# A fused attention and SwiGLU block: when the gate and up weight tiles are made, and where the second blocks' rows wait

## The chip, the cores and the metric

The kernel runs on one core of a Trainium2 chip. The metric is device time in microseconds of one execution; the time of a version is the median of its runs. Beside the timed runs there is one profiled execution, which all rows of the trace come from.

## What is computed

The reference is one adaptive-layer-norm transformer block in float32, with 2048 rows of width 576. Cut to what matters:

```python
mod = silu(c) @ w_mod                       # six vectors: sa, ca, ga, sb, cb, gb
h = layernorm(x) * (1 + ca) + sa
q = h @ wq                                  # 32 heads of 128
o = softmax(q k^T / sqrt(128)) v            # last 512 cached keys and values, 16 KV heads
x = x + ga * (o @ wo)                       # 4096 -> 576
h = layernorm(x) * (1 + cb) + sb
x = x + gb * ((silu(h @ w1) * (h @ w3)) @ w2)   # 576 -> 4608 -> 576
```

## The kernel before, in words

**Precision.** TensorE multiplies in a rounded float32 form. Every operand is therefore split into a high part (a rounded copy, by ScalarE) and a low part (operand minus high part, by VectorE or GpSimd), and three products stand for one. A product of 2 x 2 blocks is done with seven block products instead of eight (p1 to p7); for that, sums and differences of the blocks have to be made first.

**Stages.** First attention, in 128 slots i of four steps t (one slot is one head on one block of 512 rows; first both row blocks 0 and 1 over all heads, then blocks 2 and 3). Then the MLP's projections, `mlp()`, in 72 groups g: 36 feature tiles f of 128 columns, gate and up together, on the row blocks 0 and 1 (groups 0 to 35, the first pass), and the same tiles again on blocks 2 and 3 (groups 36 to 71, the second pass, which begins with tiles 35 and 34). A group has seven products k = 0 to 6 in the order p1, p2, p6, p7, p5, p3, p4 (line 554), each of seven matmuls. Between products PE does the down projection of the pair of groups before, in units of six matmuls: one unit after each of k = 0, 1, 2, 3 and 6, two after k = 4, none after k = 5 (line 962). Units write two PSUM banks by turns (pe, pf); VectorE adds each into SBUF (L904). A unit can only start when VectorE has drained the same bank two units earlier.

**What each product sets off.** After p1, ScalarE copies the bank y (L989) before p6 may add to it; after p6 likewise (L995); after p5 likewise (L998), and p3 waits for that. VectorE adds the second bank x (L991, L999, L1005) and multiplies (L1003, L1006). In odd groups VectorE also makes one low part of the activations at k = 5 (L110, with its high part by ScalarE, L109); the other low parts of activations (L110) and their sums (L943, L950, L958, L959) are GpSimd's.

**Weight tiles.** A tile f of gate and up has four blocks of 128 x 384. `load_raw(f)` (L667) brings them to SBUF; `set_piece(f, n)` (L673) makes the seven operands: GpSimd sums (L683 to L688), a high part by ScalarE (L692), a low part by GpSimd in two instructions (L697, L698). The finished 128 x 5 x 128 operand is written to DRAM (`put_out`, L703), and `load_wset` (L786) brings it back, in both passes, one operand per product, a group ahead (L1211 to L1216), into eight buffers. `set_piece` also serves the query weights. `r_item` does the same for the rows of w2, `h_item` for the activations of the families A0, A1, M0.

**What sets the order.** The order on each engine is the program's order, written out by hand: `at(i, t, task, ...)` puts a task after step t of slot i, or of group ("m", g); step -1 is ahead of the group's first product. All DMAs shown go through SyncE's queue, in order. Preparation is spread over attention's steps by a planner, `lay` (L1164): each item has pieces with costs in ns for GpSimd, and a piece goes to the first step whose pace (3300 or 3100 ns a step, less fixed work) leaves room. An item is loaded when the item before the last has ended, since two buffers hold raw data. A first list (37 items) starts at step 13, a second one at slot 68; into the second, the three M0 items are put at index 16.

**Row buffers.** Four wide buffers (tag "x", 9 KB a partition) hold either a block of rows, `acc[b]`, or raw weights. During the first pass all four hold rows: acc[0] and acc[1], which the down projection adds into, and acc[2] and acc[3], which are waiting. `spill(b)` writes rows to DRAM, `load_x(b)` brings them back, `fetch_rows(b)` brings them into other buffers for the layer norm. `split_x(pair)` (L1217) is one GpSimd subtraction over 128 x 1152 elements that the down projection of that pair of blocks needs beforehand. At the end of the first pass `finish` (L852) does five GpSimd sums per row tile.

Of the kernel before, what the change touches and what calls it, by code (L numbers as in the profile page):

```python
# [8 lines left out]
F32 = mybir.dt.float32  # L9
F32R = mybir.dt.float32r  # L10
# [7 lines left out]
P = 128  # L18
D = 576
DC = 4  # L20
DR = 64
# [8 lines left out]
NF = F // P  # L30
# [8 lines left out]
WLEAD = 4  # L39
PACE = 3300, 3100  # L40
MORE, A1_ITEM = 0, 3

ORDERED = {mybir.EngineType.PE, mybir.EngineType.DVE, mybir.EngineType.Activation, mybir.EngineType.Pool, mybir.EngineType.SP}
SCALE = float(DH) ** -0.5
# [8 lines left out]
def tile_block(  # L53
# [16 lines left out]
    nc = tc.nc  # L70
# [5 lines left out]
    pool = ctx.enter_context(tc.tile_pool(name="pool", bufs=2))  # L76
# [52 lines left out]
    acc, rows, mid = {}, {}, {}  # L129
# [424 lines left out]
    ORDER = ("p1", "p2", "p6", "p7", "p5", "p3", "p4")  # L554
# [6 lines left out]
    hd, hsets, sets = {}, {}, {}  # L561
# [77 lines left out]
    def load_set(fam, k):  # L639
# [4 lines left out]
    wdram = {  # L644
        (f, k): dram.tile([P, DC + 1, P], F32, name=f"wd{f}{k}")
        for f in (*range(NF), *(("q", g) for g in range(HKV)))
        for k in ORDER
    }
    works = {}
# [17 lines left out]
    def load_raw(f):  # L667

        whole = wide([P, 6, 3, P], "wraw")
        nc.sync.dma_start(whole[:, :4], w13[f] if isinstance(f, int) else wqs2[f[1]])  # L670
        works[f] = whole

    def set_piece(f, n):  # L673

        def views():
            return [works[f][:, k] for k in range(6)]

        k, which = (("p2", 1), ("p1", 0), ("p4", 3), ("p5", 4), ("p6", 5), ("p7", 2), ("p3", 1))[n]

        def prep():  # L680
            a11, a12, a21, a22, s1, s2 = views()
            if n == 0:
                nc.gpsimd.tensor_add(s1, a21, a22)  # L683
                nc.gpsimd.tensor_sub(s2, s1, a11)
            elif n == 1:
                nc.gpsimd.tensor_sub(a21, a11, a21)
            elif n == 6:
                nc.gpsimd.tensor_sub(a12, a12, s2)  # L688

        def high():  # L690
            x, t = views()[which], staging([P, DC + 1, P], "wmade")
            nc.scalar.copy(t[:, :3, :], x)  # L692
            return x, t

        def low(xt):
            x, t = xt
            nc.gpsimd.tensor_sub(t[:, 3:, :], x[:, :2, :], t[:, :2, :].bitcast(F32))  # L697
            nc.gpsimd.tensor_sub(t[DR:, 2, :], x[DR:, 2, :], t[DR:, 2, :].bitcast(F32))  # L698
            if n == 6:
                del works[f]  # L700

        def put_out(xt):
            nc.sync.dma_start(wdram[f, k][:, :, :], xt[1].bitcast(F32))  # L703

        return (0 if n == 6 else None, (2040, 1020, 0, 0, 0, 0, 1020)[n], 1200), (prep, high, low, put_out)

    DOWN = (("p4", "p7"), ("p6",), ("p1", "p5"), ("p2", "p3"))
    G = NF // 2
    FLIP, LAST = G, G - 2
# [2 lines left out]
        for p in range(G + 1)  # L712
        for q, ks in enumerate(DOWN)
    }
# [14 lines left out]
    def rows_pieces(p):  # L729
# [4 lines left out]
        def piece(n, k, which, last):  # L734
# [26 lines left out]
            def put_out(xt):  # L761
                to = []
                if k is not None:
                    q = next(q for q, ks in enumerate(DOWN) if k in ks)
                    to.append(odram[p, q][:, DOWN[q].index(k), :, :])
                if p == LAST and k in ("p1", None):
# [252 lines left out]
    def at(i, t, task, *args):  # L1019

        tasks.setdefault((i, t), []).append((task, args))
# [72 lines left out]
    for Q in range(PLAIN, 2 * HKV):  # L1094
        spans, at0 = (FIRST_SPANS, 16 * Q - 5) if Q == PLAIN else (SPANS, 16 * Q - 9)
        step = at0
        for k, counts in zip(ORDER_Q, spans):
            begin[Q, k] = step
            n0 = 0
            for c in counts:  # L1100
                qsteps.setdefault(step, []).append((Q, k, slice(n0, n0 + c)))
                n0, step = n0 + c, step + 1
# [50 lines left out]
    def w_item(f):  # L1153
        return (lambda: load_raw(f)), [set_piece(f, n) for n in range(7)]

    def r_item(p):
        return (lambda: load_rows(p)), rows_pieces(p)

    mlp_items = []
    for p in range(G + 1):  # L1160
        mlp_items += [w_item(f) for f in (2 * p, 2 * p + 1) if p < G]
        mlp_items.append(r_item(p))

    def lay(items, first, STEP):  # L1164
# [46 lines left out]
    for g in range(last_group):  # L1211
        for k, name in enumerate(ORDER):
            if groups[g][1] == groups[g + 1][1]:
                at(("m", g), k, keep_wset, g, name)
            else:
                at(("m", g), k, load_wset, g + 1, name)  # L1216
    def split_x(pair):  # L1217

        a = acc[2 * pair + 1]
        nc.gpsimd.tensor_sub(a[:, :, :HALF], a[:, :, :HALF], a[:, :, HALF:])  # L1220

    for d in range(2 * G):
        g = 2 * d
# [5 lines left out]
            times = ((4, (g, 2)), (3, (g, 4)))  # L1229
        for q, (i, t) in times:  # L1230
            at(("m", i), t, load_oset, d, q)
    for pair, i in ((0, ("m", 0)), (1, ("m", 14))):
        at(i, 0, split_x, pair)
    at(("m", 2), -1, begin_sums, 0)
    at(("m", 2 * G + 2), 3, begin_sums, 1)

# [60 lines left out]
    for b in (2, 3):  # L1297
        for t in range(ST):
            at(("m", b), t, norm_stats, b, t)
        at(("m", 4), 1, norm_root, b)  # L1300
    for b, g in ((2, 6), (3, 9)):
        at(("m", g), 0, norm_scale, b)
        for t in range(ST):
            at(("m", g), t, norm_rows, b, t)
        for m in range(DC + 1):
            at(("m", g + 1 + m // 3), 2 * (m % 3), store_h, "M1", b, m, "AS"[m % 2], "raw")
    at(("m", 12), -1, begin_parts, "M1")
    for c in range(3):
        g = 12 + 6 * c
# [104 lines left out]
    for k, name in enumerate(("shift", "gain")):  # L1414
        sections = wms.pop(k)
        for m in (2, 3, 0, 1, 4):
            w = sections[m]
# [26 lines left out]
    for m in range(DC + 1):  # L1444
        k = P if m < DC else DR
# [111 lines left out]
```

## Time and profile before

| | |
|---|---|
| median of 3 runs | 2955.62 us (2955.44 to 2955.67) |
| the profiled execution | 2954.41 us, its span 2952.6 us |
| PE busy | 2903.8 us (98%) |
| DVE, ACT, POOL busy | 2011.1, 1560.9, 1751.2 us |
| moved by DMA | 751.27 MB, 254 GB/s over the span |
| the M0 groups, from the first matmul of p1 | 1708.62 us on, most of them 16.73 us |

PE is TensorE, DVE VectorE, ACT ScalarE, POOL GpSimd, SP SyncE. A row of a timeline has the start in us, the duration, the engine, the line of the kernel, the operation and its tiles and, in brackets, how long the engine stood idle before it and what ended that. A row of a group has busy time, the mean duration in ns and the idle time ahead of the group's instructions. "x<-y" names the tile written and those read.

### The profile page before, as it was taken

What the parts mean: (1) busy time and instruction counts of PE and PEld (TensorE: products, weight loads), DVE (VectorE), ACT (ScalarE), POOL (GpSimd) and SP (SyncE); (2) the same over time, 40 slices, a digit from 0 to 9 for tenths busy, and PEclk for the clock granted to TensorE, in tenths of its full rate; (3) what the DMA queues carried; (4) which work ended last, traced back from release to release, by engine and by line L of the source; (5) the groups of instructions that cost most, each with busy time, mean ns of one, the idle gap of its engine ahead of it and who ended that gap; (6) DMA issues with size and microseconds to landing.
All of it is one profiled execution on the core that took longest, in us unless ns stands there. A gap on an engine that the chain in (4) does not pass through costs nothing.

```text
span 2952.6 us, 47355 instructions
## 1 busy us (share of the span) xinstructions
PE 2903.8 (98%) x16056; PEld 2384.8 (81%) x16056; DVE 2011.1 (68%) x3149; ACT 1560.9 (53%) x3251; POOL 1751.2 (59%) x1884
## 2 busy tenths in 40 slices
PE   7999999999999999999999999999999999999999
PEld 6777777777777777777777778888888888888887
DVE  7877787777777877777777766555555555555556
ACT  6667777777656776677677543333333222222322
POOL 3678888888712877777878223355564544334345
PEclk9999999999999999999999999999999999999999
DMA  6989999999885999989889946677766766666664
GB/s 216 280 266 347 277 345 311 298 289 299 260 277 179 326 301 295 296 284 283 273 278 299 300 154 202 218 233 251 251 226 202 286 231 199 205 198 193 202 201 143
DMA packets 441205, 751.27 MB, mean 254 GB/s; under 512 B 185730, under 2 KB 185730, under 8 KB 437380
## 3 DMA queue, kind: packets, MB, share of 16 engines
q1 hardware_dynamic: 440964, 748.25, 79.1%
q8 instruction: 128, 2.10, 0.3%
q14 instruction: 113, 0.93, 0.1%
HBM read 474.97 MB, written 235.37 MB: 241 GB/s over the span
## 4 chain that ended last, share of the span: by engine, by line
PE 80%; DVE 7%; ACT 4%; issue 2%; POOL 1%; DMA 1%; SPq 0%; ACTq 0%; POOLq 0%; DVEq 0%
PE py L797 15%; PE px L797 11%; PE po L530 10%; PE pe L428 10%; PE pf L910 7%; PE pe L910 7%; PE qy L797 5%; PE pt L505 4%; PE qx L797 3%; PE pss L466 2%; PE pss L468 2%; PE pss L467 2%; DVE nm L470 1%; DVE pt L515 1%; DVE acc L547 1%
## 5 line engine op out<-in xcount | busy, mean ns | idle before, releaser
L797 PE MATMUL py<-hset,wset 128*128 128x512 f32 x2016 | 507.2, 391 | 0.0
L547 DVE SCALAR_TENSOR_TENSOR acc<-pe,r,acc 128x576 f32<-128x576 f32 x510 | 413.6, 811 | 58.1 <-PE pe L428 55.4
L797 PEld LDWEIGHTS py<-hset,wset 128*128 128x128 f32 x2016 | 362.4, 188 | 59.0 <-ACT u L998 0.2
L428 PEld LDWEIGHTS pe<-o,oth 128*128 128x128 f32 x2040 | 319.7, 188 | 79.4 <-DVE acc L547 41.6
L797 PE MATMUL px<-hset,wset 128*128 128x512 f32 x1512 | 380.5, 391 | 0.0
L428 PE MATMUL pe<-o,oth 128*128 128x288 f32 x2040 | 360.1, 298 | 12.9 <-DVE acc L547 11.8
L530 PE MATMUL po<-pt,v 128*128 128x512 f16 x1536 | 353.8, 380 | 0.3 <-DMA v<-vs 0.3
L470 DVE TENSOR_REDUCE nm<-pss 128x1 f32<-128x512 f32 x512 | 345.6, 675 | 7.3 <-PE pss L468 7.1
L479 ACT ACTIVATE p<-pss,nm 128x512 f32<-128x512 f32 x384 | 265.7, 692 | 144.7 <-DVE nm L470 141.5
L697 POOL TENSOR_TENSOR wmade<-wraw,wmade 128x256 fp32r<-128x256 f32 x364 | 272.8, 749 | 115.5 <-issue 49.5
L110 POOL TENSOR_TENSOR akv<-u,akv 128x512 fp32r<-128x512 f32 x141 | 182.7, 1307 | 228.8 <-ACT akv L109 227.9
L797 PEld LDWEIGHTS px<-hset,wset 128*128 128x128 f32 x1512 | 275.5, 188 | 49.4
L509 ACT ACTIVATE pt<-pt 128x512 f16<-128x512 f32 x384 | 229.7, 598 | 136.6 <-PE pt L505 134.9
L535 DVE SCALAR_TENSOR_TENSOR otl<-po,undo,oth 128x512 fp32r<-128x512 f32 x128 | 96.1, 751 | 278.7 <-ACT oth L534 272.9
L515 DVE SCALAR_TENSOR_TENSOR pt<-pt 128x512 f16<-128x512 f32 x384 | 261.7, 681 | 28.7 <-ACT pt L509 28.3
L530 PEld LDWEIGHTS <-v 128*128 128x128 f16 x1536 | 140.6, 98 | 160.3 <-DMA v<-vs 0.6
L505 PEld LDWEIGHTS pt<-ident,p 128*128 128x128 f32 x1536 | 186.0, 140 | 72.0 <-PE pss L468 15.7
L505 PE MATMUL pt<-ident,p 128*128 128x128 f32 x1536 | 231.2, 273 | 9.4 <-DVE pt L515 6.4
L797 PE MATMUL qy<-hset,wset 128*128 128x512 f32 x784 | 237.0, 413 | 0.0
L466 PE MATMUL pss<-kh,qh 128*128 128x512 f32 x512 | 227.2, 444 | 6.3 <-ACT qh L109 2.2
L428 PE MATMUL pe<-o,otl 128*128 128x288 f32 x1020 | 217.5, 294 | 0.0
L468 PE MATMUL pss<-kh,ql 128*128 128x512 f32 x512 | 201.3, 393 | 0.9 <-DVE ql L110 0.9
(250 smaller groups left out, 5974.9 us busy)
## 6 DMA issues: line engine op xcount, KB each, us to landing
oset<-od SPq DMA_DIRECT2D x106, 576.0 KB, 4.7
od<-omade SPq DMA_DIRECT2D x133, 288.0 KB, 4.1
wraw<-in_B_w SPq DMA_DIRECT2D x36, 768.0 KB, 6.4
kept<-o SPq DMA_DIRECT2D x64, 288.0 KB, 5.1
o<-kept SPq DMA_DIRECT2D x32, 576.0 KB, 5.8
wraw<-in_A_wq_pairs SPq DMA_DIRECT2D x16, 768.0 KB, 6.3
w2raw<-in_B_w SPq DMA_DIRECT2D x38, 288.0 KB, 4.3
oset<-od SPq DMA_DIRECT2D x35, 288.0 KB, 3.2
```

Source lines behind the costliest of these rows:

```text
L428: nc.tensor.matmul(ps[:, h, :HALF], a[:, rows], b[:, h * HALF : (h + 1) * HALF], start=n == 0, stop=n == 2)
L466: nc.tensor.matmul(pss, st["qh"][:, rows], kh, start=True, stop=False)
L468: nc.tensor.matmul(pss, st["ql"][:, rows], kh, start=False, stop=True)
L470: nc.vector.tensor_reduce(nm, pss, axis=AX.X, op=ALU.max, negate=True)
L479: nc.scalar.activation(p, pss, AF.Exp, bias=nm, accum_out=st["l"][:, t : t + 1])
L505: nc.tensor.transpose(ps[:, j * P : (j + 1) * P], p[:, j * P : (j + 1) * P], ident)
L515: nc.vector.scalar_tensor_tensor(lo, p, LIFT, hi, op0=ALU.mult, op1=ALU.subtract)
L530: nc.tensor.matmul(po, v[:, d, j, :], pt[:, e, j, :], start=k == 0, stop=k == 3 * KC - 1)
L547: nc.vector.scalar_tensor_tensor(a, ps[:, :, :HALF], st["r"][:, t : t + 1], a, op0=ALU.mult, op1=ALU.add)
L697: nc.gpsimd.tensor_sub(t[:, 3:, :], x[:, :2, :], t[:, :2, :].bitcast(F32))
L797: nc.tensor.matmul(ps, w[:, a, :], h[:, b, :], start=start and n == 0, stop=n == 6, skip_group_check=True)
L910: nc.tensor.matmul(ps[:, h, :HALF], a[:, rows], w[:, b, :], start=m == 0, stop=m == 2)
```

## The change

The constant `MADE_LATE = 7` leaves tiles 0 to 6 with the planner. Tiles 7 to 35 are made during the first pass, a group ahead of their use: `make_high` (GpSimd sums and ScalarE's high part, straight into the SBUF buffer that PE reads) at step k of group f - 1, `make_low` one step later, now on VectorE, and `keep_set`, three steps after that, writes the operand to DRAM for the second pass (not for tile 35, which group 36 uses at once). `load_raw(f)` comes at step 4 of group f - 2. To have buffers for the raw tiles, acc[2] and acc[3] are spilled at group 4, fetched again for the norms at groups 5 and 8, and loaded back at groups 36 and 37; so the second pair's `split_x` moves from group 14 to step 5 of group 37. The planner's second list falls from 43 items to 14.

```diff
--- before.py
+++ after.py
@@ -39,6 +39,7 @@
 WLEAD = 4
 PACE = 3300, 3100
 MORE, A1_ITEM = 0, 3
+MADE_LATE = 7
 
 ORDERED = {mybir.EngineType.PE, mybir.EngineType.DVE, mybir.EngineType.Activation, mybir.EngineType.Pool, mybir.EngineType.SP}
 SCALE = float(DH) ** -0.5
@@ -703,6 +704,32 @@
             nc.sync.dma_start(wdram[f, k][:, :, :], xt[1].bitcast(F32))
 
         return (0 if n == 6 else None, (2040, 1020, 0, 0, 0, 0, 1020)[n], 1200), (prep, high, low, put_out)
+
+    def make_high(f, k):
+
+        a11, a12, a21, a22, s1, s2 = [works[f][:, j] for j in range(6)]
+        if k == "p1":
+            nc.gpsimd.tensor_add(s1, a21, a22)
+            nc.gpsimd.tensor_sub(s2, s1, a11)
+        elif k == "p2":
+            nc.gpsimd.tensor_sub(a21, a11, a21)
+        elif k == "p7":
+            nc.gpsimd.tensor_sub(a12, a12, s2)
+        x = {"p1": a11, "p2": a12, "p6": s2, "p7": a21, "p5": s1, "p3": a12, "p4": a22}[k]
+        t = sets[f, k] = pool.tile([P, DC + 1, P], F32R, tag="w", name="wset", bufs=8)
+        nc.scalar.copy(t[:, :3, :], x)
+        works[f, k] = x, t
+
+    def make_low(f, k):
+
+        x, t = works[f, k]
+        nc.vector.tensor_sub(t[:, 3:, :], x[:, :2, :], t[:, :2, :].bitcast(F32))
+        nc.vector.tensor_sub(t[DR:, 2, :], x[DR:, 2, :], t[DR:, 2, :].bitcast(F32))
+        if k == ORDER[-1]:
+            del works[f]
+
+    def keep_set(f, k):
+        nc.sync.dma_start(wdram[f, k][:, :, :], works.pop((f, k))[1].bitcast(F32))
 
     DOWN = (("p4", "p7"), ("p6",), ("p1", "p5"), ("p2", "p3"))
     G = NF // 2
@@ -1158,7 +1185,7 @@
 
     mlp_items = []
     for p in range(G + 1):
-        mlp_items += [w_item(f) for f in (2 * p, 2 * p + 1) if p < G]
+        mlp_items += [w_item(f) for f in (2 * p, 2 * p + 1) if f < MADE_LATE]
         mlp_items.append(r_item(p))
 
     def lay(items, first, STEP):
@@ -1212,8 +1239,15 @@
         for k, name in enumerate(ORDER):
             if groups[g][1] == groups[g + 1][1]:
                 at(("m", g), k, keep_wset, g, name)
+            elif MADE_LATE <= g + 1 < NF:
+                for late, task in enumerate((make_high, make_low, keep_set)[: 2 + (g + 2 < NF)]):
+                    m, step = divmod(8 * g + k + 1 + late * late, 8)
+                    at(("m", m), step - 1, task, g + 1, name)
             else:
                 at(("m", g), k, load_wset, g + 1, name)
+    for f in range(MADE_LATE, NF):
+        at(("m", f - 2), 4, load_raw, f)
+
     def split_x(pair):
 
         a = acc[2 * pair + 1]
@@ -1229,8 +1263,8 @@
             times = ((4, (g, 2)), (3, (g, 4)))
         for q, (i, t) in times:
             at(("m", i), t, load_oset, d, q)
-    for pair, i in ((0, ("m", 0)), (1, ("m", 14))):
-        at(i, 0, split_x, pair)
+    for pair, i in ((0, ("m", 0)), (1, ("m", NF + 1))):
+        at(i, 5 * pair, split_x, pair)
     at(("m", 2), -1, begin_sums, 0)
     at(("m", 2 * G + 2), 3, begin_sums, 1)
 
@@ -1298,12 +1332,16 @@
         for t in range(ST):
             at(("m", b), t, norm_stats, b, t)
         at(("m", 4), 1, norm_root, b)
+        at(("m", 4), 2, spill, b)
+        at(("m", NF + b - 2), (4, 0)[b - 2], load_x, b)
     for b, g in ((2, 6), (3, 9)):
+        at(("m", g - 1), 4, fetch_rows, b)
         at(("m", g), 0, norm_scale, b)
         for t in range(ST):
             at(("m", g), t, norm_rows, b, t)
         for m in range(DC + 1):
             at(("m", g + 1 + m // 3), 2 * (m % 3), store_h, "M1", b, m, "AS"[m % 2], "raw")
+        at(("m", g + 2), 3, rows.pop, b)
     at(("m", 12), -1, begin_parts, "M1")
     for c in range(3):
         g = 12 + 6 * c
```

## The prediction

> **What bounds the kernel now.** I read the page's head first, then busy time in stretches of 100 us, then the chain of waits for the attention half, then the engines' timelines around one group of the projections.
>
> The stretches (columns: PE with its count, weight loads, DVE, ACT, POOL, granted clock, DMA share, GB/s):
>
> ```profile
> span 2952.6 us, 47355 instructions
> 800.00:900.00 100.00, 99.62 (x563) 77.85 (x562) 75.06 (x123) 57.70 (x121) 11.72 (x8) 1.00 0.76 235
> 1500.00:1600.00 100.00, 98.91 (x559) 77.42 (x557) 74.15 (x119) 70.62 (x161) 82.03 (x109) 1.00 0.94 295
> 2100.00:2200.00 100.00, 100.00 (x546) 88.30 (x545) 55.60 (x76) 32.38 (x59) 60.31 (x46) 1.00 0.70 231
> 2600.00:2700.00 100.00, 100.00 (x546) 88.26 (x546) 54.78 (x76) 29.10 (x51) 39.68 (x30) 1.00 0.63 200
> ```
>
> PE bounds everything, at a full clock. What attention loses to preparation is small: 563 matmuls in 100 us without it (POOL 12%), 559 with it (POOL 82%). In the projections PE has no gap at all. So a change that moves POOL, ACT and DMA work can win only attention's few lost matmuls, and can lose wherever it makes the gapless PE wait.
>
> **Attention: what leaves, and what it was costing.** The rows of the chain that mark a slot's twelve matmuls with the values:
>
> ```profile
> 896.36 2.62 PE po L530 x12
> 947.68 2.62 PE po L530 x12
> ...
> 1211.73 2.62 PE po L530 x12
> 1265.92 2.62 PE po L530 x12
> ...
> 1680.01 2.62 PE po L530 x12
> ```
>
> Four slots without preparation take 947.68 - 896.36 = 51.32 us: the floor. The planner's list for the second half shrinks from 43 items to 14 (eleven row items, three of the M0 family). I worked its arithmetic through: at 3100 ns a step a row item takes five steps, so eleven from step 272 reach about 327, and the M0 items end at step 347, slot 87. Counting PE's groups of twelve, slot 68, where this list begins, has its group at 947.68, and slot 88 has it at 1211.73: from there on nothing is prepared any more. Before, the last ends at step 486, slot 121.5. The list is too short for index 16, so the M0 items come last. From 1265.92 to 1680.01 are 32 slots, 414.09 us; at the floor 8 x 51.32 = 410.56. So **-3.5 us**, and this loss has a name: DVE late in draining the output bank.
>
> ```profile
> PEld pe L428 <- DVE acc L547: 13.7, 31, 1.1
> ACT hst L1131 <- DMA hdM0p<-hst: 2.4, 1, 2.4
> PEld pt L505 <- DVE p L515: 2.2, 1, 2.2
> ```
>
> The first row covers 960 to 1680 us, the other two 1225 to 1279. The four slots from 1211.73 took 54.19, 2.9 over the floor. They hold the M0 family's last items, and ACT's wait for a staging buffer held DVE and then PE. Those items move to slots 82 to 87 and may meet the same wait there, beside fewer transfers: I take a third of it, **-1.0**; ends 0 and -2.9. In the first half three weight items become row items, of similar length: 0, with a rival below.
>
> **What comes into the first pass.** Per tile, from the rows grouped by form:
>
> ```profile
> L697 POOL TENSOR_TENSOR wmade<-wraw,wmade 128x256 fp32r<-128x256 f32 x364 | 272.8, 749 | 115.5 <-issue 49.5 <-ACT wmade L692 45.3 <-POOL wmade L698 5.4
> L692 ACT CAST wmade<-wraw 128x384 fp32r<-128x384 f32 x364 | 173.1, 512 | 2.5 <-POOL wraw L688 1.6 <-DMA od<-omade 0.6 <-POOL wmade L697 0.4
> L698 POOL TENSOR_TENSOR wmade<-wraw,wmade 64x128 fp32r<-64x128 f32 x364 | 170.2, 467 | 28.6
> L686 POOL TENSOR_TENSOR wraw<-wraw 128x384 f32<-128x384 f32 x52 | 53.2, 1023 | 1.3
> ```
>
> POOL takes four sums, 4 x 1.02 = 4.1 us per group; ACT seven casts, 7 x 0.51 = 3.6; and DVE, which did none of this before, fourteen low parts in place of POOL's 749 and 467 ns. A group lasts 16.73 us (below), so POOL goes from 10.1 busy to 14.2 while the M1 family is combined, ACT from 5.4 to 9.0. ACT's critical copy is L998 between p5 and p3, with two output units of PE over it; the casts before it have the p7 product and a unit: 0, as long as POOL's sums are a step ahead.
>
> DVE's low parts no row shows. From L1005 (0.68 us for 512 columns) and L904 (0.74 for 576), quoted next, a column costs 0.94 ns and an instruction 0.2: an estimate of 0.44 + 0.32, and 0.62 in a queue whose instructions overlap by 0.07. Seven pairs are 4.3 us on top of 0.556 x 16.73 = 9.3: 13.6 of 16.73, which fits on the average. But the place decides, and POOL. Around the start of group 30 (2225.70):
>
> ```profile
> 2224.97 1.30 POOL L958 TENSOR_TENSOR u<-u,u 128x512 f32<-128x512 f32 x1 [2.09 <-DVE u L1003]
> 2226.35 1.62 POOL L959 TENSOR_TENSOR u<-u,u 128x512 f32<-128x512 f32 x1
> ...
> 2225.58 1.23 DVE L110 TENSOR_TENSOR aal<-u,aah 128x512 fp32r<-128x512 f32 x1 [0.69 <-ACT aah L109]
> 2226.74 0.68 DVE L1005 TENSOR_TENSOR u<-px,u 128x512 f32<-128x512 f32 x1
> 2227.45 1.06 DVE L1006 TENSOR_TENSOR u<-u,s 128x512 f32<-128x512 f32 x1
> 2228.44 0.74 DVE L904 TENSOR_TENSOR acc<-pe,acc 128x576 f32<-128x576 f32 x1
> ...
> 2225.70 1.76 PE L797 MATMUL py<-hset,wset 128*128 128x512 f32 x7
> 2229.69 0.42 PE L910 MATMUL pe<-oset,aah 128*128 128x288 f32 x2
> 2242.42 1.76 PE L797 MATMUL py<-hset,wset 128*128 128x512 f32 x7
> ...
> 2243.19 0.75 DVE L904 TENSOR_TENSOR sums<-pf,sums 128x576 f32<-128x576 f32 x1
> 2246.41 0.96 PE L910 MATMUL pf<-oset,akv 128*128 128x288 f32 x6
> ...
> 2058.32 0.69 DVE L110 TENSOR_TENSOR aal<-u,aah 128x512 fp32r<-128x512 f32 x1 [0.69 <-ACT aah L109]
> ```
>
> The unit at 2229.69 writes bank pe, which L904 drains until 2228.44 + 0.74 = 2229.18: **0.5 us to spare**. In an odd group the change puts p5's low pair on DVE behind L110 (step 5), ahead of L1005, L1006 and that drain. Undisturbed that is +0.62, a stall of 0.1. But DVE work with both inputs in SBUF meets POOL's: the same L110 took 0.69 once and 1.23 here beside L958, and L959 took 1.62 against L958's 1.30, while L1005, which reads PSUM, did not stretch. So the first low part, at 2226.74, finds L959 holding SBUF until about 2227.9 and ends at 2228.2. Then POOL's two new sums for the next tile stand ready behind L959. If they miss the second low part, L1006 meets them once, the drain ends near 2230.5 and the stall is 0.85. If POOL gets in between each time, the second low part ends near 2229.2, L1006 near 2230.7, the drain near 2231.3: 1.65. I take 1.25, nearer to the blocked row, since POOL now has work queued there. It happens at 14 starts of even groups (8, 10, ... 34): 14 x 1.25 = **+17.5** (ends 14 x 0.1 = 1.4 and 14 x 1.65 = 23). At the start of an odd group (31, at 2242.42) L110 is missing and the same drain ends at 2243.94 for a unit at 2246.41, 2.5 us to spare, more than the 1.65 just worked out: 0.
>
> The Trainium skill, page "SBUF — State Buffer", section "Who interferes with whom", says that a VectorE instruction with two SBUF inputs and a GpSimd one that reads SBUF exclude each other for the whole instruction, whichever issues first. By it alone the sum takes the 1.65 and the change's low parts are in the wrong engine while POOL is busy; the rows agree that there is a block, and leave open whether it is held to the last nanosecond.
>
> **Queues and transfers.** SP gives up seven tile loads per group and gets seven stores and one raw load of 768 KB.
>
> ```profile
> DMA packets 38294, 92.82 MB, mean 232 GB/s; under 512 B 4431, under 2 KB 4431, under 8 KB 38265
> wraw<-in_B_w SPq DMA_DIRECT2D x36, 768.0 KB, 6.4
> ```
>
> From 1900 to 2300 us the first pass moves 232 GB/s; 768 KB in 16.73 us add 47, to 279, under the 295 of attention above. A store waits for a low part issued three steps earlier, so neither SP nor the output-weight loads behind it stand. The raw load is issued at step 4 of the group before and needed from step 0 of the next, three steps of 16.73 / 7 = 2.4 us, 7.2, against 6.4 to landing: 0; if it is late by 1, ACT, at 9.0 of 16.73, has room. The second blocks' rows go out at group 4, come back once for the norms and once around group 36, 2.4 MB each time, all of it several steps ahead of its first reader: 0, ends 0 and +2.
>
> **The pass boundary.** The second pair's split moves from group 14, where PE saw nothing of it, to group 37.
>
> ```profile
> L1220 POOL TENSOR_TENSOR acc<-acc x2: 2672/2682/2693, 1702.8 to 1962.9; 128x1152 f32<-128x1152 f32 x2
> ...
> 2371.12 1.27 POOL L110 TENSOR_TENSOR aal<-u,aah 128x512 fp32r<-128x512 f32 x1
> ...
> 2372.45 0.40 PE L910 MATMUL pf<-oset,aal 128*128 128x288 f32 x1 [0.87 <-POOL aal L110]
> 2373.73 0.53 PE L910 MATMUL pe<-oset,aah 128*128 128x288 f32 x2 [0.48 <-DVE acc L904]
> ```
>
> There POOL is queued without a gap from the finishing sums on, and PE already waits for it. Another 2.68 us in that queue lands on PE: **+2.7** (ends 0 and 4).
>
> Sum: -3.5 - 1.0 + 17.5 + 2.7 = +15.7. The profiled execution took 2954.41 us, its span 2952.6; it becomes 2970.1. The runs' median, 2955.62, is 1.2 above it: **2971**. A difference of 0.2%, 5.9 us, is about what I call a change.
>
> **Rivals.** (1) *Nothing to see.* The low parts find gaps in POOL, or the drain's half microsecond and a slightly cheaper low part are enough: 0.1 to 0.3 at 14 starts, 3 us. For it: 13.6 of 16.73 fits. Against it: POOL's new sums are queued just there. Then -4.5 + 3 + 2.7 = +1: 2957. (2) *Faster.* Preparation in attention costs more than the floor shows after 1212 us: the row items that replace three weight items at slots 36 to 50 load POOL and the staging buffers less. The page's total for the L428 wait on L547 is
>
> ```profile
> PEld pe L428 <- DVE acc L547: 41.6, 79, 1.2
> ```
>
> so 41.6 - 13.7 = 27.9 lie mostly before 960; over some 14 of 65 slots that is 6. If it goes, with the whole 2.9 and no stall in the first pass: -3.5 - 2.9 - 6 + 2.7 = -9.7, 2946. It decides once the 14 starts cost under 4 us together. Against it: three items of fifteen change and the pace is the same. (3) *SBUF's shared side becomes the bound.* If blocks last as long as busy times, POOL's 14.2 and DVE's two-input work (7 x 0.76 low parts, L1003, L1006 and every other L110, about 7) need 21.2 of 16.73 in the 18 groups with combining, and 0.397 x 16.73 + 4.1 + 7 = 17.7 in the other ten: 18 x 4.5 + 10 x 1.0 = +91, 3045. This is that section's rule taken to the letter. Against it: L1006 of group 31 started inside a POOL instruction's last 0.17 us and was not stretched, so the hold ends before the busy time does:
>
> ```profile
> 2241.43 1.29 POOL L110 TENSOR_TENSOR akv<-u,akv 128x512 fp32r<-128x512 f32 x1 [4.05 <-ACT akv L109]
> 2242.55 0.71 DVE L1006 TENSOR_TENSOR u<-u,s 128x512 f32<-128x512 f32 x1
> ```
>
> **How the numbers follow.** The forecast has 0.57 (own range 2961 to 2984, its ends 14 x 0.85 and 14 x 1.65 with the small terms), rival 1 0.27, rival 2 0.11, rival 3 0.05. Faster 0.11; same 0.29, with a little of the forecast's low end; slower 0.60. The range 2950 to 2988 leaves out most of rival 2, rival 3 and the forecast's upper tail.
>
> **What would show it.** Right: slots from 88 on at 51.3 per four; even groups 8 to 34 of the first pass longer than 16.73 by about a microsecond, PE idle before bank pe's first unit with DVE L904 as releaser, odd groups at 16.73; PE's wait for POOL's aal at the boundary near 3.5 us instead of 0.87. Wrong: every group at 16.73 (rival 1), or ACT's L998 late behind a cast that waits for POOL, or a raw tile that lands late.

## The result, and the profile after

| | before | after |
|---|---|---|
| median | 2955.64 us (2955.44 to 2957.45, 4 runs) | 3053.30 us (3050.47 to 3056.59, 4 runs) |
| ratio after / before | | 1.0329, 95% interval 1.0311 to 1.0347 |
| the profiled execution, its span | 2954.41, 2952.6 us | 3056.59, 3054.8 us |
| first matmul of p1 of group 0 | at 1708.62 us | at 1705.32 us |
| first pass, group 0 to the start of group 36 | 617.44 us | 718.01 us |
| groups 36 to 38 | 52.56 us | 57.57 us |
| group 39 to the end | 573.97 us | 573.81 us |

The change is 3.3% slower. The spans differ by 102.2 us: attention gave back 3.3, the first pass took 100.6 more and the boundary 5.0 more, and what follows is 0.2 shorter. Where the pass loses it, in the stretches shown of before (PE, weight loads, DVE, ACT, POOL, granted clock, DMA share, GB/s):

```profile
span 3054.8 us, 46757 instructions
2100.00:2200.00 100.00, 86.76 (x436) 73.59 (x435) 94.52 (x128) 39.44 (x80) 69.31 (x55) 0.95 0.70 237
2600.00:2700.00 100.00, 100.00 (x546) 88.22 (x545) 54.93 (x75) 28.91 (x51) 39.29 (x31) 1.00 0.63 199
```

Between 2100 and 2200 us PE does 436 matmuls instead of 546, and VectorE, which was at 56%, stands at 95%. GpSimd has only gone from 60 to 69%. DMA is as busy as before. In the second pass everything is as it was. So VectorE has become the bound, and the groups of its instructions say with what (count, busy us, mean ns):

```profile
L726 DVE TENSOR_TENSOR wset<-wraw,wset 128x256 fp32r<-128x256 f32 x203 | 157.6, 776 | 0.9
L727 DVE TENSOR_TENSOR wset<-wraw,wset 64x128 fp32r<-64x128 f32 x203 | 144.2, 710 | 2.7
```

The second instruction has a fourth of the first one's elements and takes nearly as long. By line, the shortest, middle and longest of each, in ns:

```profile
L726 DVE TENSOR_TENSOR wset<-wraw,wset x203: 407/722/1555, 1822.5 to 2411.3; 128x256 fp32r<-128x256 f32 x102
...
L727 DVE TENSOR_TENSOR wset<-wraw,wset x203: 287/292/1428, 1822.9 to 2411.8; 64x128 fp32r<-64x128 f32 x102
```

Their work is 0.41 and 0.29 us; the rest is waiting inside the instruction, and the trace shows for what. Of the 203 L726, 125 began while a GpSimd instruction was running. 122 of these were stretched, and every one of them ended 0.28 to 0.29 us after that GpSimd instruction did. Of the 203 L727, 103 began so, and 101 were stretched and ended 0.15 us after it (the five that began so and went free: four in its last 0.17 us, one for no reason that I can name). No other one was stretched. So VectorE is stopped until the GpSimd instruction is all but over, and not merely slowed down; only about 0.13 us of the two can overlap (0.41 - 0.28, and 0.29 - 0.15 gives the same). In 135 of the 203 pairs at least one of the two was held, and 68 pairs went free.

One place, the start of group 30 (p1 at 2309.62), on VectorE, GpSimd and PE:

```profile
2309.79 1.23 DVE L111 TENSOR_TENSOR aal<-u,aah 128x512 fp32r<-128x512 f32 x1 [0.69 <-ACT aah L110]
2310.95 1.51 DVE L726 TENSOR_TENSOR wset<-wraw,wset 128x256 fp32r<-128x256 f32 x1
2312.46 1.01 DVE L727 TENSOR_TENSOR wset<-wraw,wset 64x128 fp32r<-64x128 f32 x1
2313.51 0.69 DVE L1032 TENSOR_TENSOR u<-px,u 128x512 f32<-128x512 f32 x1
2314.23 0.72 DVE L1033 TENSOR_TENSOR u<-u,s 128x512 f32<-128x512 f32 x1
2314.88 0.74 DVE L931 TENSOR_TENSOR acc<-pe,acc 128x576 f32<-128x576 f32 x1
2315.54 0.41 DVE L726 TENSOR_TENSOR wset<-wraw,wset 128x256 fp32r<-128x256 f32 x1
2315.96 0.29 DVE L727 TENSOR_TENSOR wset<-wraw,wset 64x128 fp32r<-64x128 f32 x1
...
2310.55 1.62 POOL L986 TENSOR_TENSOR u<-u,u 128x512 f32<-128x512 f32 x1
2312.13 1.20 POOL L712 TENSOR_TENSOR wraw<-wraw 128x384 f32<-128x384 f32 x1
2313.40 1.00 POOL L713 TENSOR_TENSOR wraw<-wraw 128x384 f32<-128x384 f32 x1
...
2315.67 0.53 PE L937 MATMUL pe<-oset,aah 128*128 128x288 f32 x2 [1.90 <-DVE acc L931]
```

The two engines alternate: L726 begins while GpSimd has L986 and takes 1.51, L727 takes 1.01 beside the new sum L712, and the pair at 2315.54, with GpSimd idle, takes 0.41 and 0.29. PE waits 1.90 us for the drain behind them. That is the place and the mechanism that the prediction named, a little dearer than its 1.65. But it is one place of many. Over the first pass from group 6 on, PE waited for (total us, times, longest):

```profile
PE pe L937 <- DVE sums L931: 29.8, 14, 2.6
PE pe L937 <- DVE acc L931: 19.5, 11, 2.7
PE pf L937 <- DVE sums L931: 9.9, 6, 2.9
PE pf L937 <- DVE acc L931: 8.7, 6, 2.5
```

68 us of waiting, and each of these rows is for a drain. Over the whole first pass PE's rows have it idle 71.3 us longer than before, and at work 29.3 us longer on the same 3363 matmuls; part of the second figure is the granted clock (below). Of the waits most stand before the unit after p2 in even groups (11 times, 19.5 us) and before the unit after p6 in odd groups (15 times, 30.0 us). The even groups 8 to 34 took 274.99 us instead of 236.55, the odd ones 7 to 33 took 295.90.

### The profile page after: what moved, and what is told of

It is laid out like the page before. It is cut to its first block, busy times and chain, and to the rows that moved or that the text cites. A ratio compares the mean times of both kernels' runs of the same rounds, so it can differ in the third digit from the quotient of the medians.

```text
span 3054.8 us, 46757 instructions
## 1 busy us (share of the span) xinstructions
PE 2935.1 (96%) x16056; PEld 2397.8 (78%) x16056; DVE 2294.3 (75%) x3555; ACT 1566.8 (51%) x3251; POOL 1518.2 (50%) x1478
## 4 chain that ended last, share of the span: by engine, by line
PE 69%; DVE 14%; ACT 4%; issue 4%; DMA 3%; POOL 2%; SPq 1%; DVEq 0%; ACTq 0%; POOLq 0%
PE py L824 11%; PE pe L429 10%; PE po L531 10%; PE px L824 8%; PE pe L937 5%; PE pf L937 5%; PE qy L824 4%; PE pt L506 4%; PE qx L824 3%; PE pss L467 3%; PE pss L469 2%; PE pss L468 2%; DVE wset L727 2%; DVE wset L726 2%; DVE pt L516 1%
## 5 line engine op out<-in xcount | busy, mean ns | idle before, releaser
L824 PE MATMUL px<-hset,wset 128*128 128x512 f32 x1512 | 391.3, 399 | 2.9 <-DVE u L1026 1.5
L824 PEld LDWEIGHTS px<-hset,wset 128*128 128x128 f32 x1512 | 282.7, 193 | 55.6 <-DVE u L1026 2.0
L118 POOL TENSOR_TENSOR ql<-qv,qh 128x512 fp32r<-128x512 f32 x28 | 36.1, 1290 | 563.1 <-ACT qh L117 562.8
L111 POOL TENSOR_TENSOR akv<-u,akv 128x512 fp32r<-128x512 f32 x141 | 186.8, 1335 | 176.0 <-ACT akv L110 165.1
L1019 ACT ACTIVATE s<-s 128x512 f32<-128x512 f32 x72 | 45.6, 633 | 305.3 <-DVE s L1018 305.3
```

Of the source, the lines that this page charges most:

```text
L111: eng.tensor_sub(lo, src, hi.bitcast(F32))
L824: nc.tensor.matmul(ps, w[:, a, :], h[:, b, :], start=start and n == 0, stop=n == 6, skip_group_check=True)
```

## The experiments

Theory A: VectorE's low parts, which read two SBUF operands, and GpSimd's instructions keep each other out of SBUF; that doubles the low parts and makes VectorE the bound of the first pass. Theory B: fourteen more instructions a group, standing in front of VectorE's drains, are the cost, whatever they read. Theory C: GpSimd's four new sums make what is queued behind them late. A theory D came up with the trace, on the granted clock. The kernel before, run beside them, had medians of 2956.51 to 2957.14 us.

**One SBUF operand instead of two**

```diff
-        nc.vector.tensor_sub(t[:, 3:, :], x[:, :2, :], t[:, :2, :].bitcast(F32))
-        nc.vector.tensor_sub(t[DR:, 2, :], x[DR:, 2, :], t[DR:, 2, :].bitcast(F32))
+        wide_in = t[:, :2, :].bitcast(F32).rearrange("p a (n o) -> p a n o", o=1)
+        nc.vector.tensor_reduce(t[:, 3:, :], wide_in, axis=AX.X, op=ALU.max)
+        tail = t[DR:, 2, :].bitcast(F32).rearrange("p (n o) -> p n o", o=1)
+        nc.vector.tensor_reduce(t[DR:, 2, :], tail, axis=AX.X, op=ALU.max)
```

> The 14 low-part instructions per group keep their engine, place, size and number, but each reads one SBUF operand instead of two (a reduction over an axis of length one of the high part: the low parts are not computed, their places get the high part). Theory A (a VectorE instruction with two SBUF inputs and a GpSimd one exclude each other; 203 pairs took 776 + 710 ns where the undisturbed ones took about 410 + 290): VectorE falls from 20 us a group to about 14.5 of 16.73, the first pass from 718 back to 617 to 630 us, the span to 2955 to 2965. Theory B (fourteen more instructions in front of VectorE's drains, whatever they read): the first pass stays above 690, the span above 3025. Theory C (GpSimd's four new sums make everything behind them late): stays near 3050.

Measured: 2963.42 us, 1.0021 of before (1.0011 to 1.0030); profiled span 2957.4, first pass 623.98 us. The groups:

```profile
L727 DVE TENSOR_REDUCE wset<-wset 128x256 fp32r<-128x256 f32 x203 | 83.1, 409 | 0.9
L729 DVE TENSOR_REDUCE wset<-wset 64x128 fp32r<-64x128 f32 x203 | 57.4, 283 | 2.8
```

Same engine, places, number and sizes, and 0.69 us a pair instead of 1.49; the durations of VectorE's instructions add up to 14.84 us a group in groups 12 to 29 instead of 20.56, and 94 of the 100.6 us are gone. B and C fall as main causes. What stays is 6.5 us, all of it in even groups (0.6 to 1.2 us in eight of the 14, nearly nothing in the others). That is what the place alone costs.

**Without the sums**

```diff
-        if k == "p1":
-            nc.gpsimd.tensor_add(s1, a21, a22)
-            nc.gpsimd.tensor_sub(s2, s1, a11)
...
-        x = {"p1": a11, "p2": a12, "p6": s2, "p7": a21, "p5": s1, "p3": a12, "p4": a22}[k]
+        x = {"p1": a11, "p2": a12, "p6": a11, "p7": a21, "p5": a21, "p3": a12, "p4": a22}[k]
```

> GpSimd's four sums per late tile are left out (the operands that need them take a raw block instead), the low parts on VectorE stay. A: GpSimd has 4 us a group less to meet the low parts with, so a third to a half of the 100 us goes: span 3000 to 3020, and the low parts' mean falls from 776 and 710 to about 600 and 500 ns. B: nothing changes, 3045 to 3055. C: nearly all of it goes, 2960.

Measured: one run, 3002.96 us, first pass 665.78: half of the loss is gone.

```profile
L719 DVE TENSOR_TENSOR wset<-wraw,wset 128x256 fp32r<-128x256 f32 x203 | 132.4, 652 | 0.9
L720 DVE TENSOR_TENSOR wset<-wraw,wset 64x128 fp32r<-64x128 f32 x203 | 120.0, 591 | 2.7
```

As A has it, though the low parts shrink less than expected: they meet the activations' low parts and sums, which GpSimd had all along, as well as the new ones.

**The low parts back on GpSimd**

```diff
-        nc.vector.tensor_sub(t[:, 3:, :], ...
-        nc.vector.tensor_sub(t[DR:, 2, :], ...
+        nc.gpsimd.tensor_sub(t[:, 3:, :], ...
+        nc.gpsimd.tensor_sub(t[DR:, 2, :], ...
```

> The late tiles' low parts go back to GpSimd, at the same steps. A: VectorE is free, but GpSimd would need 11.5 + 4.1 + 8.5 = 24.1 us a group in groups 12 to 29 and 6.9 + 12.6 = 19.5 in the others, of 16.73: 7.4 x 18 + 2.8 x 11 = 164 us more in the first pass, span about 3110. B: the drains stand free, 2960 to 2975.

Measured: one run, 3118.97 us; the first pass 783.55, 166.1 over before where 164 were worked out. That the total agrees so well is luck in part: groups 12 to 29 took 23.55 us on the mean instead of 24.1, groups 7 to 11 and 30 to 34 took 21.5 instead of 19.5.

```profile
2100.00:2200.00 100.00, 84.42 (x398) 71.76 (x397) 38.98 (x54) 38.69 (x76) 94.67 (x108) 0.88 0.57 202
```

GpSimd is the bound, at 95%, and VectorE falls to 39%. VectorE was the better of the two engines for the low parts, and not good enough.

**One low part on each engine**

```diff
-        nc.vector.tensor_sub(t[DR:, 2, :], x[DR:, 2, :], t[DR:, 2, :].bitcast(F32))
+        nc.gpsimd.tensor_sub(t[DR:, 2, :], x[DR:, 2, :], t[DR:, 2, :].bitcast(F32))
```

> The first low part (128 x 256) stays on VectorE, the second (64 x 128) goes to GpSimd. A (what counts is the time that VectorE's two-input work and GpSimd's work hold together, whichever engine has it): GpSimd gets 7 x 0.49 = 3.4 us a group, 19 in groups 12 to 29 before any waiting, VectorE loses its second low part: between the two versions in the groups without combining, still about 20 us in the others, first pass 680 to 710, span 3015 to 3045. If VectorE's count of instructions were the matter: first pass under 650.

Measured: one run, 3000.22 us, first pass 664.67. That is better than either version of one engine, and better than A's sum allowed; it is not B's either. Groups 12 to 29 take 19.05 us, groups 30 to 34 17.51.

```profile
2100.00:2200.00 100.00, 90.47 (x467) 77.06 (x468) 77.96 (x102) 44.94 (x89) 93.91 (x96) 0.98 0.75 258
```

GpSimd is again the bound, VectorE has room. So it isn't right to add both engines' busy times as if SBUF had one door for all of them: counted that way, with 0.467 us (L698) on GpSimd in place of the estimated 0.32 on VectorE seven times, a group with combining would have needed 1.0 us more than with both low parts on VectorE, and it took 1.9 us less (19.05 instead of 20.94).

**Drains ahead of low parts**

```diff
+                after = (0, {"p5": 2, "p4": 2}.get(name, 1), 4)
-                    m, step = divmod(8 * g + k + 1 + late * late, 8)
+                    m, step = divmod(8 * g + k + 1 + after[late], 8)
```

> The low parts of p5 and p4 come one step later, so that every drain of an output bank stands ahead of the low parts of its step; nothing else changes. A: VectorE stays the bound, 98% busy: the first pass 705 to 720, span above 3040. B (the place in front of the drains): the first pass falls to 630 or less, span under 2970.

Measured: one run, 3031.62 us, first pass 696.49. Between the two: 21.5 us were a matter of place, more than A left for it, and 79 stay, with VectorE at 97%.

```profile
2100.00:2200.00 100.00, 90.07 (x465) 74.29 (x465) 96.89 (x133) 41.98 (x85) 73.03 (x59) 1.00 0.71 242
```

**Five late tiles only** (`MADE_LATE = 31`)

> Only tiles 31 to 35 are late, so only groups 30 to 34 make tiles, and there GpSimd combines nothing for the M1 family. A (the price is paid group by group, where low parts meet GpSimd): these five at 18.5 to 21 us, mean 19.3 as in the changed kernel, all groups before at 16.73; first pass 617.4 + 13 = 630. If lateness builds up over the pass instead: well under 19 on the mean, first pass under 625.

Measured: one run, 2972.20 us, first pass 628.08; groups 0 to 30 at their old lengths, 31 to 35 20.40, 18.61, 19.41, 18.61 and 17.23. Over the five groups expected the mean is 18.75, a little under the 19.30 of the changed kernel. The price is paid on the spot, from the second group that makes tiles on.

**The rows alone** (`MADE_LATE = NF`), the split a group earlier, and no split at all

> All 36 tiles are made during attention as before; only the second blocks' rows are spilled, fetched and loaded back, and the second pair's split stands in group 37. If the 5.0 us that groups 36 to 38 became longer come from the split in GpSimd's queue: first pass 617, groups 36 to 38 57.6 us, span 2957 to 2958. If they were left over from the first pass's lateness: 2953. If spill and refetch cost something of their own, the first pass is over 617.4.

```diff
-    for pair, i in ((0, ("m", 0)), (1, ("m", NF + 1))):
-        at(i, 5 * pair, split_x, pair)
+    for pair, i, t in ((0, ("m", 0), 0), (1, ("m", NF), 2)):
+        at(i, t, split_x, pair)
...
-        at(("m", NF + b - 2), (4, 0)[b - 2], load_x, b)
+        at(("m", NF - 3 + b), (4, 4)[b - 2] if b == 2 else -1, load_x, b)
```

> As the version that only moves the rows, but the blocks are loaded back from step 4 of group 35 on and the second pair's split stands at step 2 of group 36, where GpSimd still has idle time. If the split's place in GpSimd's queue is what groups 36 to 38 pay for: 52.6 us again instead of 55.1, span about 2.6 below that version's. If it is the eight loads beside the second pass's activations: still 55.

```diff
-    for pair, i in ((0, ("m", 0)), (1, ("m", NF + 1))):
-        at(i, 5 * pair, split_x, pair)
+    at(("m", 0), 0, split_x, 0)
```

> The version that only moves the rows, with the second pair's split left out (the second blocks' output is wrong). If the split's 2.67 us in GpSimd's queue are what groups 36 to 38 pay for: 52.6 us there, as before the change. If the loads of the rows are: 55.1.

Measured, rows alone: 2962.00 us, 1.0016 of before (1.0007 to 1.0026); first pass 617.45, so spill and refetch cost nothing there; groups 36 to 38 55.14 us, 2.58 over before. The median is 4.9 us over before, more than that: in the profile the first pass starts 2.95 us later too (1711.57), though this version changes nothing in attention. The two versions below start it at 1710.2, so attention alone differs by up to 3 us from profile to profile. The split a group earlier: 2963.07, 1.0022 (1.0012 to 1.0031), groups 36 to 38 58.49, worse. No split: one run, 2956.23, groups 36 to 38 52.55, as before the change. PE's longest waits at the boundary, for the rows alone, the early split and no split:

```profile
2378.00 0.40 PE L937 MATMUL pf<-oset,aal 128*128 128x288 f32 x1 [2.23 <-POOL aal L111]
```

```profile
2347.32 1.02 PE L937 MATMUL pf<-oset,akv 128*128 128x288 f32 x6 [3.43 <-DMA oset<-od]
```

```profile
2374.01 0.40 PE L937 MATMUL pf<-oset,aal 128*128 128x288 f32 x1 [0.85 <-POOL aal L111]
```

The split's 2.67 us in GpSimd's queue are what the boundary pays for. Moving it forward failed for two reasons. The loads then join the queue behind the second pass's activations, and a load of output weights behind them comes late: that is the 3.43. And the split itself waits for its rows: GpSimd stood idle for 8.39 us until 2345.13, 17.5 us into group 36, with the rest of its queue behind, and PE's wait for L111 two groups later was 2.23 us again, as with the late split.

**Place and operand together, and the early split** (the diffs of the first, the fifth and the early-split experiment in one)

> Three things together: low parts that read one SBUF operand (so they are not computed), drains ahead of low parts, the split at group 36. With the meeting gone, place is what is left: the 6.5 us that the starts of even groups kept should go, the first pass 617 to 618, groups 36 to 38 52.6, span 2949 to 2954. It is the most that the change could have won. If the first pass stays near 624, the 6.5 us have another cause than the low part in front of the drain.

Measured: 2959.33 us, 1.0010 of before (1.0001 to 1.0020); first pass 618.50, so 5.5 of the 6.5 us were the low part in front of the drain; groups 36 to 38 60.29, the early split's fault again. With the late split's 55.14 in its place the profiled span, 2957.9, would be 2952.7, before's 2952.6; the median would be 2954.2, and before's beside it was 2956.5. This is an estimate, no run has that combination. Even without the meeting and with the best place, then, attention's gain and the split about cancel, within 2 us.

**Filling PE's idle stretches**

After some of PE's long waits the granted clock falls. The changed kernel around 2085 us, PE's rows, then the stretch of the fall:

```profile
2085.18 1.06 PE L937 MATMUL pe<-oset,akv 128*128 128x288 f32 x6 [2.62 <-DVE sums L931]
2086.08 2.99 PE L824 MATMUL px<-hset,wset 128*128 128x512 f32 x7
```

```profile
2086.30:2089.70 3.40, 3.40 (x11) 2.81 (x10) 3.07 (x6) 2.32 (x6) 1.53 (x2) 0.50 0.91 298
```

Seven matmuls that take 1.76 us take 2.99. It happens eleven times in the first pass, 11 x 3.41 us at half clock: 18.8 us of PE's work.

```diff
+                if MADE_LATE - 1 < g < NF - 1 and name == ("p2", "p6")[g % 2]:
+                    to = st["x"] if name == "p2" else st["y"]
+                    for _ in range(4):
+                        w, h = sets[g, name], hsets["M0", name]
+                        nc.tensor.matmul(to, w[:, 2, :], h[:, 2, :], start=False, stop=True, skip_group_check=True)
```

> The changed kernel with four extra matmuls a group in groups 7 to 34, repeating the last one of p2 in even groups and of p6 in odd ones, just ahead of the units that wait longest (the products come out wrong). Theory D (idle stretches of over about 2 us make the granted clock fall to half for 3.4 us, 11 times in the first pass, and that is worth up to 11 x 1.7 = 19 us): idle stretches become 0.9 us shorter, the clock falls at most 3 times, and the span comes out 8 to 18 us shorter than the changed kernel's although PE has 25 us more to do. If the fallen clock costs nothing, since PE waits for VectorE anyway: the same time or up to 10 us longer, with the falls gone. If the falls do not hang on the idle stretches: still about 11.

> The changed kernel as it is, on the chip of the three runs before it, to compare them with: 3050 to 3057.

Measured: the changed kernel again 3056.38 us (3051.86 to 3058.17), filled 3049.28 (3046.43 to 3051.45), 1.0333 (1.0316 to 1.0351) and 1.0310 (1.0295 to 1.0326) of before. The clock falls 6 times in the first pass instead of 12, and the pass takes 711.0 us instead of 718.2, with 112 more matmuls in it. Fewer falls, and some time back for more work, as D has it, but the falls were halved and not ended, and the gain is 7 us where 8 to 18 were expected. How much of the first pass's loss the clock is in all stays open. The sum has 18.8 us of PE's own work; the 7 us that came back need not be the clock alone, since the extra matmuls can also shift which instructions of VectorE and GpSimd meet.

## Why the prediction was wrong

**Attention, -4.5.** Right in mechanism, and in size as far as the spread allows. From slot 88 on four slots take the floor:

```profile
1214.52 2.62 PE po L531 x12
1265.82 2.62 PE po L531 x12
...
1625.32 2.62 PE po L531 x12
```

51.30 us, and 359.50 for the next 28 slots, 51.36 per four. The pass starts 3.3 us earlier: of the -3.5, 3.2 us are there over the same 32 slots, and the M0 family's wait came again in its new place (in both profiles ACT waits 3.5 us in all for the staging buffers). But attention differs by some 3 us between profiles: the nine profiles with seven tiles made early start the pass at 1703.1 to 1707.2 us, the four with all 36 at 1708.6 to 1711.6, and the means are 5.2 apart (the one with 31 starts it at 1713.3). So -4.5 is within what the runs show, and its split into -3.5 and -1.0 is not settled.

**The boundary, +2.7.** Right: 2.58 with the rows alone, and nothing without the split. In the changed kernel's profile it was 5.0, because there the clock fell for 6.8 us; in its second profile, without that fall, 55.16 - 52.56 = 2.6. The sign that was given for it, a wait of 3.5 us for GpSimd's aal, came out at 2.23; another 0.73 stands at a drain shortly before.

**The queues and transfers, 0.** Right: 617.45 us with all the row traffic, and PE's waits in the first pass name no transfer.

**The first pass, +17.5.** This is the step that failed, at 100.6. Its mechanism, at the place where I looked, was right: low parts meet GpSimd's instructions, the drain is late, PE waits 1.90 us at the unit after p2. Wrong was to price the meeting at that one place and to say of the rest that 13.6 of 16.73 us "fits on the average". That average took all seven pairs undisturbed, at 0.62 and 4.3 us in all; I let one pair in a group be held up and six go free. Two thirds of all pairs are held, and in groups 12 to 29 a pair takes 1.57 us on the mean, seven of them 11.0. The rest of VectorE's work takes 9.6, where the sum had 9.3, and together that is the 20.56 measured. Over 16.73 it isn't late at a place any more but is the bound, and PE's wait moves to wherever a drain comes due. So the 0 for odd groups fell too: they lost more than the even ones, 59.4 us against 38.4, since there the drain of the unit after p1 stands behind the low parts of p3 and p4. The low end was too small as well: with the meeting gone the place alone cost 6.5 us, not 14 x 0.1 = 1.4.

**The rivals.** The third had the cause and nearly the number: 21.2 us a group with combining and 17.7 without, 3045 us; measured 20.94, 19.30 and 3053. I gave it 0.05, because one instruction that began within the last 0.17 us of a GpSimd one was not stretched. That showed that the two can overlap a little at the end (0.13 us, by the rows after the change); it was no reason to doubt the hold. Its sum is right by luck in part: it adds both engines' busy times, and the version with one low part on each engine shows that this is too much. The nearest row was at hand: L110 on VectorE took 1171 ns on the mean against 692 undisturbed. Its 0.48 us more, set against seven pairs in place of one, makes 13.6 + 3.4 = 17.0, over the 16.73 already with one low part of each pair held. The upper end of the forecast's own range, 2984, is some 3 us more than its terms add up to; nothing rests on it.

The Trainium skill, page "SBUF — State Buffer", section "Who interferes with whom", was to be taken seriously: two-input VectorE instructions and GpSimd ones that read SBUF block each other, one-input VectorE instructions outside the two-port modes don't. The runs agree with both halves, 409 and 283 ns with one input against 776 and 710 with two.

## What to carry to other kernels

When work moves to an engine that "has room", add it to that engine's busy time at the price it has beside its new neighbours, for every instruction of the period and not at the tightest place alone; if the sum comes near the period, the engine is the new bound and the place doesn't matter. Here VectorE work with two SBUF inputs came to about double: 1.57 us a pair against 0.69, beside a GpSimd that was 68% busy. And ask first what can be won: the work taken out of attention had been costing 3 to 5 us there, since PE hid it, so hardly anything that it cost elsewhere could be paid for.

## What the runs showed of the hardware

The granted clock falls to half after PE waits that are shorter than the 3.4 us it then stays down: in the changed kernel each fall in the first pass follows a wait of 2.1 to 2.7 us (twelve waits of over 2 us were followed by a fall, the boundary's counted, six were not, the longest of these 2.93 us). The Trainium skill, page "TensorE: Matmul & The Clock Gate", section "What's actually happening", puts the fall after an idle window of about 3.4 us; here no wait was that long, so the measurement decides. Which waits count can be read from the trace: the twelve falls of groups 0 to 38 start on one grid of 3.413 us. Cut along that grid, the stretch just before each fall has PE idle for 1.91 to 2.69 us, and of all other stretches only one has over 1.76 (1.92). The six long waits without a fall each lie across a line of the grid; the longest is cut into 1.45 and 1.48. So a bound engine that lets PE idle for 2 us at a time can cost more than the idle time.

A VectorE reduction over an axis of length one, from SBUF to SBUF, took 409 ns for 256 columns beside a GpSimd that was 83% busy from 2100 to 2200 us, as short as the two-input instruction takes alone (407 at its shortest).
